# Four-layer attention chain on one core: feature maps, reciprocals, first keys and three residuals computed in another way, with new instruction orders

## The chip, the core and the metric

One Trainium2 chip, one of its cores. A core has five engines with a queue of instructions each: PE (TensorE, matrix products into PSUM), ACT (ScalarE), DVE (VectorE), POOL (GpSimd) and SP (SyncE, which here only issues transfers). They run side by side and wait for each other by semaphores; each takes its own instructions strictly in order. The metric is the time of one launch on the device, in microseconds (us), as the median of several runs.

## The reference

Four residual layers, A, B, A, B, over a sequence of 2048 rows of 512 numbers (bf16), 32 heads of 16. Both layers of a kind use the same weights.

```python
def A(x, wqkv, wo):                     # linear attention
    q, k, v = split(x @ wqkv)           # heads of 16
    phi = lambda t: where(t > 0, t + 1, exp(t)) + 1e-6
    pq, pk = phi(q), phi(k)
    kv = einsum("bhsd,bhse->bhde", pk, v)
    z = einsum("bhsd->bhd", pk)
    num = einsum("bhqd,bhde->bhqe", pq, kv)
    den = einsum("bhqd,bhd->bhq", pq, z)[..., None] + 1e-6
    return (num / den) @ wo

def B(x, wqkv, wo):                     # causal attention, window of 256
    q, k, v = split(x @ wqkv)
    p = softmax(where(mask, q @ k.T * 0.25, -1e9))
    return (p @ v) @ wo

x = x + A(layernorm(x)); x = x + B(layernorm(x))
x = x + A(layernorm(x)); x = x + B(layernorm(x))
```

## The kernel before

The 2048 rows lie in SBUF as 16 tiles of 128 rows (xres, bf16). The work falls into five stretches that overlap at their edges:

1. the first layer's keys: each tile is normalised (`norm`: statistics, mean and variance on DVE, `eps` and `pow` on POOL, the scaled tile `xn` on DVE), transposed by PE for tiles 0 to 4 and by a transfer for the others, multiplied by the weights of keys and queries (`a_k`, `a_q`), and sent through the feature map `phi`;
2. the first middle stretch: for each tile the end of layer A (`a_out`, residual `resid`), the layer norm, layer B's queries, keys and values (`b_qkv`, `b_v`), scores (`b_scores`, `b_first`, `b_far`), exponentials on ACT, masks, the product with the values (`b_values`), the output product (`b_out`), the residual, the next layer norm, and the second layer A's keys and values;
3. the change-over (`barrier`): the sums over all tiles (`a_kv`), the remaining queries, the matrix M, and for each group G of four tiles the denominators `den`, their reciprocals `rec`, and `spread`, a product that repeats each reciprocal over the 16 columns of its head;
4. the second middle stretch, the same as the first with the last layer B; it writes the finished tiles out;
5. the tail: the last two tiles' values, output products, residuals and stores (`b_last` for tile 15).

Nothing in the program looks for parallelism while it runs. A planner was run beforehand, and its result is the packed `TABLE`: one order of all instructions, the engine of each instruction that could run on two (a copy out of PSUM may be on ACT or DVE, a far mask on DVE or POOL, a store on POOL or SP), and the PSUM bank of each product. `place` unpacks it, and `synchronise` derives the semaphore waits. The keys and parameters in the text (`PAR`) have no further effect on the order. The eight PSUM banks are reused all the time: a product waits until the readers of the bank's last content are done.

The parts that the change touches:

- `phi` has two forms. The plain one: `E` (exponential, ACT, PSUM to tE), `E1` (minimum with 1, plus 1e-6, DVE), `phi` (plus 1 and maximum, DVE, which reads the product from PSUM and tE). The form with `near`: ACT makes two passes over the product, `E` and `R` (plus 1, into XQ), and DVE takes the maximum `mx` of two SBUF tiles. `BY_ACT` lists the query tiles with the second form: 0 to 6 for the first layer A, 4 to 8 for the second.
- the product of a query tile with its spread reciprocals: `pqd` on DVE straight from PSUM, or, for the groups in `COPIED`, a copy `sc` into tE (ACT or DVE) and a product `pm` of two SBUF tiles on DVE. `COPIED` holds group 0 of the first and groups 0 and 1 of the second layer A.
- the keys of layer B are stored twice, once with the odd and once with the even rows zero. For most tiles `bke` copies them out of PSUM and two transfers `kd` place them; for the tiles in `NEAR` (tile 0 of both layers B) two passes `kz` over PSUM write them directly, each scaled by a column of zeros and ones.
- `tok` is the product of a tile of rows with a matrix of 512 columns, four matmuls of 512 columns in two halves; `resid` adds it to xres on DVE. `WHOLE`, which would put the residual into the product, is empty.
- `LAST` says how many of the last tiles of a layer B have their attention output transposed by PE rather than by a transfer: 1 in the first layer B, 2 in the second.

Of the kernel before, what the change touches and what calls it, by code (L numbers as in the profile page):

```python
# [9 lines left out]
ALU = mybir.AluOpType  # L10

P = 128
# [223 lines left out]
class Plan:  # L236
# [173 lines left out]
    def tok(self, name, t, lhs, rhs, rd, key, whole=False):  # L410
# [3 lines left out]
        if whole:  # L414
            self.pe("id", lambda e: e.matmul(K.ps(ps), K.ident[:], K.xres[:, t, :], start=True, stop=False), key - 0.01, 1, 512, rd=[("xres", t), ("ident",)], ps=[ps])
        for h in range(2):
            def put(e, h=h):
                m = None
                for c in (2 * h, 2 * h + 1):
                    m = e.matmul(K.ps(ps), lhs(c), rhs(c), start=c == 0 and not whole, stop=c == 3)  # L420
                return m
            self.pe(name, put, key - 0.001 * h, 2, 512, rd=rd, ps=[ps])
# [417 lines left out]
    def b_out(self, j, key, by_pe, whole=False):  # L840
# [4 lines left out]
        if whole:  # L845
            return po
        self.resid(j, po, key + 0.05)

    def b_last(self, j, key):
# [4 lines left out]
        for h in range(2):  # L854
# [10 lines left out]
            for n in range(2) if h else [None]:  # L865
                cs = slice(0, D) if n is None else slice(256 * n, 256 * n + 256)

                def put(e, h=h, cs=cs):
                    m = None
                    for f in (h, h + 2):  # L870
                        m = e.matmul(K.ps(po)[:, cs], K.oT[:, s, f, :], K.wBo[:, f, cs], start=f == 0, stop=f == 3, skip_group_check=True)
                    return m

                self.pe("bout", put, key + 0.1 * h + 0.01 * (n or 0), 2, cs.stop - cs.start, rd=[("oT", s, h), ("wBo",)], ps=[po])
        for n in range(2):
            cs = slice(256 * n, 256 * n + 256)
            self.on("DVE", "res", lambda e, cs=cs: e.tensor_tensor(K.xres[:, j, cs], K.ps(po)[:, cs], K.xres[:, j, cs], ALU.add), key + 0.2 + 0.1 * n, dve(256), rd=[("xres", j)], wr=[("xres", j, n)], ps=[po])
# [291 lines left out]
```

## Time and profile before

| | |
|---|---|
| median of 3 runs | 412.12 us (411.43 to 413.2) |
| the profiled execution | 412.6 us, span 410.8 us |
| instructions in the span | 17540 |
| busy: PE / DVE / ACT / POOL | 386.9 / 344.5 / 352.8 / 122.4 us |
| granted PE clock | full in every slice |
| exponentials and copies of scores, ACT (line 686) | 216 instructions, 198.9 us |
| chain that ended last, by engine | PE 51%, ACT 34%, DVE 9%, DMA 3% |

The span is what the hardware profiler saw; the execution's own time is 1.8 us longer. Busy times of ACT, DVE and POOL are the union of their instructions' times. Matmuls are pipelined, so one matmul's listed time is longer than the step from one to the next, and PE's busy time alone does not say how full PE is. The chain is followed backwards from the last instruction, at each step to what released it or to the instruction ahead of it on its engine.

### The profile page before, as it was taken

The numbers are of one execution on the slowest core, as the hardware profiler recorded it, in microseconds if no ns is written. First come the engines' busy times: TensorE is split into PE (matmuls) and PEld (weight loads), VectorE is DVE, ScalarE is ACT, GpSimd is POOL, SyncE is SP. The second block draws the span as 40 slices with busy tenths as digits, with TensorE's granted clock in tenths as the row PEclk, the third lists the DMA queues.
The fourth block names the chain that finished last, engine by engine and source line by source line (L and its number), as shares of the span: only waits on it lengthen the run. The fifth ranks groups of instructions, "written<-read, shape, count | busy, mean of one in ns | idle before, by whom it ended". The sixth has DMA issues, their size and how long they took to land.

```text
span 410.8 us, 17540 instructions
## 1 busy us (share of the span) xinstructions
PE 386.9 (94%) x7668; PEld 260.3 (63%) x7742; DVE 344.5 (84%) x807; ACT 352.8 (86%) x448; POOL 122.4 (30%) x216
## 2 busy tenths in 40 slices
PE   7999999999999999999999999999999988999896
PEld 3654676766575576566567777586757755566674
DVE  6997799989998899888887789997899688857585
ACT  4654659998999999999998357999999999999993
POOL 4576653111252331320503203303113304303020
PEclk9999999999999999999999999999999999999999
DMA  7495114443243435353222100344314821561751
GB/s 249 101 217 144 49 34 115 120 70 90 56 106 74 119 77 107 81 119 82 68 41 57 27 2 2 105 109 81 102 44 122 122 66 41 120 127 56 168 107 42
DMA packets 66596, 37.19 MB, mean 91 GB/s; under 512 B 47640, under 2 KB 61848, under 8 KB 66520
## 3 DMA queue, kind: packets, MB, share of 16 engines
q1 hardware_dynamic: 66032, 34.75, 37.0%
q8 instruction: 61, 1.00, 1.1%
q0 software_dynamic: 480, 1.31, 1.0%
q14 instruction: 15, 0.12, 0.1%
q10 hardware_dynamic: 8, 0.00, 0.0%
HBM read 6.29 MB, written 2.10 MB: 20 GB/s over the span
## 4 chain that ended last, share of the span: by engine, by line
PE 51%; ACT 34%; DVE 9%; DMA 3%; issue 2%; SPq 1%; POOL 1%
ACT pb L686 20%; PE ps L420 18%; PE ps L434 10%; PE ps L822 10%; PE ps L676 5%; ACT pb L801 5%; ACT vp L686 4%; PE ps L501 3%; ACT tE L444 2%; DMA wA<-in_A_wqkv_dram 2%; DMA xT<-xn 1%; DVE xres L604 1%; DVE stats L374 1%; ACT pb L721 1%; PE ps L477 1%
## 5 line engine op out<-in xcount | busy, mean ns | idle before, releaser
L686 ACT ACTIVATE pb<-ps 128x1024 bf16<-128x1024 f32 (+2 forms) x216 | 198.9, 1020 | 5.2 <-PE ps L676 3.9
L822 PEld LDWEIGHTS ps<-vB,pb 128*128 128x128 bf16 x2560 | 77.7, 96 | 12.3 <-DVE pb L694 3.6
L822 PE MATMUL ps<-vB,pb 128*128 128x34 bf16 x2560 | 83.5, 177 | 0.6 <-POOL pb L772 0.3
L434 PE MATMUL ps<-xT,wBp 128*128 128x128 bf16 x1024 | 69.0, 219 | 1.7 <-ACT tE L444 0.6
L434 PEld LDWEIGHTS ps<-xT,wBp 128*128 128x128 bf16 x1024 | 58.5, 98 | 13.7 <-issue 4.4
L379 POOL TENSOR_SCALAR ve<-mv 128x1 f32<-128x1 f32 x63 | 16.7, 265 | 154.7 <-DVE mv L375 152.7
L444 ACT ACTIVATE tE<-ps 128x512 bf16<-128x512 f32 x64 | 38.6, 612 | 27.1 <-PE ps L420 11.2
L772 POOL TENSOR_SCALAR_AFFINE_SELECT pb<-pb 128x1024 bf16<-128x1024 bf16 x30 | 34.4, 1146 | 71.4 <-DVE pb L694 23.8
L676 PE MATMUL ps<-XQ,kB 32*128 32x256 bf16 (+3 forms) x992 | 48.0, 267 | 3.3 <-ACT pb L754 0.7
L604 DVE TENSOR_TENSOR xres<-ps,xres 128x512 bf16<-128x512 f32 x63 | 43.0, 684 | 6.7 <-PE ps L420 6.3
L420 PE MATMUL ps<-wA,XQ 128*128 128x512 bf16 x174 | 45.6, 379 | 2.2 <-issue 0.6
L374 DVE BATCH_NORM_STATS2 stats<-xres 128x6 f32<-128x512 bf16 x64 | 43.5, 685 | 2.8 <-DMA xres<-in_A_x_dram 2.2
L694 DVE TENSOR_TENSOR pb<-pb,tri 128x512 bf16<-128x512 bf16 (+1 forms) x108 | 41.5, 396 | 3.3 <-ACT pb L686 3.1
L801 ACT ACTIVATE pb<-ps 128x1024 bf16<-128x1024 f32 x42 | 41.4, 1059 | 1.1 <-PE ps L792 0.9
L380 POOL TENSOR_TENSOR rs<-ve,negh 128x1 f32<-128x1 f32 x64 | 37.8, 591 | 8.3 <-DVE ve L377 3.0
L434 PE MATMUL ps<-XQ,wA 128*128 128x128 bf16 x512 | 35.4, 219 | 0.3 <-DMA wA<-in_A_wqkv_dram 0.3
L434 PEld LDWEIGHTS ps<-XQ,wA 128*128 128x128 bf16 x512 | 30.7, 98 | 7.3 <-DMA wA<-in_A_wqkv_dram 0.8
L420 PE MATMUL ps<-wBv,xT 128*128 128x512 bf16 x110 | 31.4, 380 | 2.6 <-issue 1.0
L676 PEld LDWEIGHTS ps<-XQ,kB 32*128 32x128 bf16 x992 | 15.0, 92 | 29.5 <-ACT pb L686 7.5
L420 PE MATMUL ps<-M,XQ 128*128 128x512 bf16 x113 | 30.7, 380 | 2.3 <-ACT vp L686 0.4
L420 PE MATMUL ps<-wBo,oT 128*128 128x512 bf16 x105 | 28.8, 380 | 2.8 <-issue 1.0
L686 ACT ACTIVATE vp<-ps 128x1024 bf16<-128x1024 f32 (+2 forms) x32 | 26.7, 928 | 1.5 <-PE ps L676 1.5
(126 smaller groups left out, 551.6 us busy)
## 6 DMA issues: line engine op xcount, KB each, us to landing
vB<-vS SPq DMA_DIRECT2D x64, 136.0 KB, 2.7
kB<-vp SPq DMA_DIRECT2D x60, 128.0 KB, 2.3
wA<-in_A_wqkv_dram SPq DMA_DIRECT2D x3, 512.0 KB, 5.5
out_dram<-xres POOLq DMA_DIRECT2D x10, 128.0 KB, 2.8
xres<-in_A_x_dram SPq DMA_DIRECT2D x2, 512.0 KB, 5.1
pb<-in_B_wqkv_dram SPq DMA_DIRECT2D x1, 1024.0 KB, 5.8
xres<-in_A_x_dram SPq DMA_DIRECT2D x3, 256.0 KB, 5.5
out_dram<-xres SPq DMA_DIRECT2D x5, 128.0 KB, 2.7
```

What stands on the lines that cost most here:

```text
L374: self.on("DVE", "stats", lambda e: e.bn_stats(K.stats[:, t, :], x()), key, dve(512), rd=rd, wr=[("stats", t)], **held)
L380: self.pow = self.on("POOL", "pow", lambda e: e.tensor_tensor(K.rs[:, t, :], K.ve[:, t, :], K.negh[:], ALU.pow), key + 0.03, (640, 690), r ...
L420: m = e.matmul(K.ps(ps), lhs(c), rhs(c), start=c == 0 and not whole, stop=c == 3)
L434: m = e.matmul(K.ps(ps)[:, f * P:(f + 1) * P], w(c, f), xT(c), start=c == 0, stop=c == 3)
L444: self.on("ACT", "E", lambda e: e.activation(K.tE[:, s, :], K.ps(ps), ACT.Exp, bias=0.0), key, act(512), wr=[("tE", s)], ps=[ps])
L604: self.on("DVE", "res", lambda e: e.tensor_tensor(K.xres[:, t, :], K.ps(po), K.xres[:, t, :], ALU.add), key, dve(512), rd=[("xres", t)], w ...
L676: m = e.matmul(K.ps(ps[gq])[:, ns * i:ns * i + ns], K.kB[rows, j % 4, 2 * f + b, :, :], K.XQ[rows, f, q:q + ns], start=True, stop=True, ti ...
L686: return e.activation(out(2 * h, 2, ns), i, ACT.Exp, bias=0.0, scale=0.25)
L694: return e.tensor_tensor(x, x, K.tri[:, 0, sh:64].unsqueeze(1).unsqueeze(1).to_broadcast([P, 4, n, 64 - sh]), ALU.mult)
L772: return e.affine_select(out=x, in_=x, compare_op=ALU.is_ge, fill=0.0, base=-2, pattern=[[0, 16], [-2, 64]], channel_multiplier=1)
L801: return e.activation(far(h), i, ACT.Exp, bias=0.0, scale=0.25)
L822: m = e.matmul(K.ps(ps)[:, 34 * u:34 * u + 34], K.P((b // 2) % rp)[:, gq, f, o:o + P], K.vB[:, (b // 2) % 4, b % 2, r, :], start=i == 0, s ...
```

## The change

Five edits in the text:

- `BY_ACT` becomes empty: all 64 feature maps take the plain form.
- `COPIED` becomes empty: every spread reciprocal is read from PSUM by `pqd`.
- `NEAR` becomes empty: tile 0's keys go the way of the others, `bke` and two transfers, in both layers B.
- the residual of tiles 13, 14 (by `WHOLE`) and of half of tile 15 in the last layer is added inside the product, by a matmul of the identity with xres that accumulates into the same bank, and a plain copy `rs` writes the sum back. For tile 15 the other half stays an addition on DVE, the copy is ordered behind it, and one store of 128 KB takes the place of two of 64 KB.
- `LAST` of the second layer B falls from 2 to 1: tile 14's attention output is transposed by a transfer.

`TABLE` is replaced: the order, the engine of each free instruction and all banks are new. Counted over the program, ACT loses 19 of 447 instructions and DVE 13 of 806; five far masks move from DVE to POOL, and PE has three matmuls more for the residuals and four transposing ones fewer.

```diff
--- before.py
+++ after.py
@@ -215,13 +215,13 @@
 LATE = 5
 KEEP = 0
 MASKS = 0
-WHOLE = {2: (), 3: ()}
+WHOLE = {2: (), 3: (13, 14)}
 FIRST = {2: 0, 3: 0}
-BY_ACT = {2: (0, 1, 2, 3, 4, 5, 6), 3: (4, 5, 6, 7, 8)}
-COPIED = {2: (0,), 3: (0, 1)}
-LAST = {2: 1, 3: 2}
+BY_ACT = {2: (), 3: ()}
+COPIED = {2: (), 3: ()}
+LAST = {2: 1, 3: 1}
 PART = (2, 3)
-NEAR = (0,)
+NEAR = ()
 PACK = {3: (9, 10, 11, 12, 13, )}
 QUAD = ()
 SUMMED = ()
@@ -411,15 +411,18 @@
 
         K = self
         ps = Tile(1, K.cls)
-        if whole:
-            self.pe("id", lambda e: e.matmul(K.ps(ps), K.ident[:], K.xres[:, t, :], start=True, stop=False), key - 0.01, 1, 512, rd=[("xres", t), ("ident",)], ps=[ps])
         for h in range(2):
             def put(e, h=h):
                 m = None
                 for c in (2 * h, 2 * h + 1):
-                    m = e.matmul(K.ps(ps), lhs(c), rhs(c), start=c == 0 and not whole, stop=c == 3)
+                    m = e.matmul(K.ps(ps), lhs(c), rhs(c), start=c == 0, stop=c == 3 and not whole)
+                if whole and h:
+                    m = e.matmul(K.ps(ps), K.ident[:], K.xres[:, t, :], start=False, stop=True)
                 return m
-            self.pe(name, put, key - 0.001 * h, 2, 512, rd=rd, ps=[ps])
+            if whole and h:
+                self.pe(name + "i", put, key - 0.001 * h, 3, 512, rd=rd + [("xres", t), ("ident",)], ps=[ps])
+            else:
+                self.pe(name, put, key - 0.001 * h, 2, 512, rd=rd, ps=[ps])
         return ps
 
     def feat(self, name, t, w, xT, rd, key):
@@ -591,16 +594,17 @@
                 self.on("DVE", "pqd", lambda e, x=x, b=bc[tg]: e.tensor_tensor(x(), K.ps(b).rearrange("p (f n) -> p f n", f=4), x(), ALU.mult), k + 0.3 + 0.01 * tg, dve(512), rd=[("XQ", t)], wr=[("XQ", t)], ps=[bc[tg]])
 
 
-    def a_out(self, t, key, whole):
+    def a_out(self, t, key):
         K = self
         x = lambda f: K.XQ[:, f, t * P:(t + 1) * P]
-        po = self.tok("aout", t, x, lambda f: K.M[:, f, :], [("XQ", t)] + [("M", f) for f in range(4)], key + 0.1, whole)
+        po = self.tok("aout", t, x, lambda f: K.M[:, f, :], [("XQ", t)] + [("M", f) for f in range(4)], key + 0.1)
+        self.resid(t, po, key + 0.15)
+
+    def resid(self, t, po, key, whole=False):
+        K = self
         if whole:
-            return po
-        self.resid(t, po, key + 0.15)
-
-    def resid(self, t, po, key):
-        K = self
+            self.copy("rs", po, lambda: K.xres[:, t, :], lambda: K.ps(po), key, 512, wr=[("xres", t)])
+            return
         self.on("DVE", "res", lambda e: e.tensor_tensor(K.xres[:, t, :], K.ps(po), K.xres[:, t, :], ALU.add), key, dve(512), rd=[("xres", t)], wr=[("xres", t)], ps=[po])
 
     def b_qkv(self, t, s, key, key2):
@@ -842,9 +846,7 @@
         s = j % 2
         self.transpose("oT", lambda: K.o[:, s, :], lambda: K.oT[:, s, :, :], [("o", s, 0), ("o", s, 1)], [("oT", s)], key - 0.15, by_pe)
         po = self.tok("bout", j, lambda f: K.oT[:, s, f, :], lambda f: K.wBo[:, f, :], [("oT", s), ("wBo",)], key, whole)
-        if whole:
-            return po
-        self.resid(j, po, key + 0.05)
+        self.resid(j, po, key + 0.05, whole)
 
     def b_last(self, j, key):
 
@@ -869,13 +871,17 @@
                     m = None
                     for f in (h, h + 2):
                         m = e.matmul(K.ps(po)[:, cs], K.oT[:, s, f, :], K.wBo[:, f, cs], start=f == 0, stop=f == 3, skip_group_check=True)
+                    if not h:
+                        m = e.matmul(K.ps(po)[:, 256:512], K.ident[:], K.xres[:, j, 256:512], start=False, stop=False, skip_group_check=True)
                     return m
 
-                self.pe("bout", put, key + 0.1 * h + 0.01 * (n or 0), 2, cs.stop - cs.start, rd=[("oT", s, h), ("wBo",)], ps=[po])
-        for n in range(2):
-            cs = slice(256 * n, 256 * n + 256)
-            self.on("DVE", "res", lambda e, cs=cs: e.tensor_tensor(K.xres[:, j, cs], K.ps(po)[:, cs], K.xres[:, j, cs], ALU.add), key + 0.2 + 0.1 * n, dve(256), rd=[("xres", j)], wr=[("xres", j, n)], ps=[po])
-            self.on("SP", "out", lambda e, cs=cs: e.dma_start(K.out[0, j * P:(j + 1) * P, cs], K.xres[:, j, cs]), key + 0.3 + 0.1 * n, (520, 2400), rd=[("xres", j, n)])
+                if h:
+                    self.pe("bout", put, key + 0.1 * h + 0.01 * (n or 0), 2, cs.stop - cs.start, rd=[("oT", s, h), ("wBo",)], ps=[po])
+                else:
+                    self.pe("boutj", put, key, 3, 512, rd=[("oT", s, h), ("wBo",), ("xres", j), ("ident",)], ps=[po])
+        self.on("DVE", "res", lambda e: e.tensor_tensor(K.xres[:, j, 0:256], K.ps(po)[:, 0:256], K.xres[:, j, 0:256], ALU.add), key + 0.2, dve(256), rd=[("xres", j)], wr=[("xres", j, 0)], ps=[po])
+        self.copy("rs", po, lambda: K.xres[:, j, 256:512], lambda: K.ps(po)[:, 256:512], key + 0.3, 256, rd=[("xres", j)], wr=[("xres", j, 1)])
+        self.on("SP", "out", lambda e: e.dma_start(K.out[0, j * P:(j + 1) * P, :], K.xres[:, j, :]), key + 0.4, (520, 2400), rd=[("xres", j, 0), ("xres", j, 1)])
 
     def phase(self, ph):
 
@@ -898,7 +904,7 @@
 
         def front(t):
             k = base + t
-            po = self.a_out(t, k - par["k_ao"], t in WHOLE[ph])
+            po = self.a_out(t, k - par["k_ao"])
             self.norm(t, k - par["k_ao"] + 0.3, t % ring, lambda: K.xT[:, t % ring, :, :], [("xT", t % ring)], t < max(par["pe_first"], FIRST[ph]), po)
             self.b_qkv(t, t % ring, k - par["k_q"], k - par["k_kv"])
 
@@ -952,60 +958,59 @@
 TABLE = (
...
 )
```

More of the change, by code (lines that the diff above doesn't have):

```diff
@@ L1007 @@
[L1007 to L1008 removed]
+    r"c-qxh1GFv4lFd*?=Cf_vwr$(CZQHhO+qP|W_e0y9bI$Fa_5b|tp7;Crnzg3xJ*TRoB6jT95t-{$Bx6hzgGLM+FwqT}7$&AkWvq#1Qk%#owi#m5nCJeLA8OK?",
+    r"I3}+dW}f-D=81pm^O+ZZxJhU7n-M0x>1ba13?`l_V2YYfCcY_XI-BVxqse5t7&S9YSCiDtG?|SvyUj?`%_K0hOb)ZsbT`RN7L(JgGJ8yNGux~-g-lj6$Mi6T",
+    r"O;3~1tT8FfDAV7pHHl0vv(7X%)l4sQ)-*E%Om5TM>^0%dIn&!DF?mdBlijp1qfH-k-i$FV%>|R#WHT4dShLUEH?2%%Gtl%k(ae5R%#1U0%>gsWj5n=K4b#sI",
@@ L1009 @@
+    r"SWl2k&>qk(tnknP1^gr!iX14+hR6om64u$^8VJp0U>W?@6bw-aL~>BfKs%MglnjnX;30*&761ih4XwanIib-HoB3b?fu)3@RzX++p~eI+DX{Q@tql_@Wc^J{",
+    r"pwPkyrVf36i-iCK37e;2w?kto7`FOC(-F2TzywyT3AB;%zW@>cD^U",
 )
```

102 lines of the change are left out of this document (48 added, 54 removed).

## The prediction

> **What bounds the kernel now.** I read four views in this order: busy time of each engine, busy time by stretch (columns: engine busy times with instruction counts, granted clock, DMA share, GB/s), the groups of PE within one stretch, and what ACT waited for.
>
> ```profile
> PE 386.9 (94%) x7668; PEld 260.3 (63%) x7742; DVE 344.5 (84%) x807; ACT 352.8 (86%) x448; POOL 122.4 (30%) x216
> ```
> ```profile
> 0.00:62.90 62.90, 59.65 (x600) 35.48 (x610) 53.64 (x135) 33.80 (x58) 37.16 (x80) 1.00 0.50 133
> 62.90:218.80 155.90, 148.92 (x3087) 98.93 (x3117) 138.13 (x320) 151.17 (x176) 40.88 (x69) 1.00 0.39 87
> 218.80:259.00 40.20, 39.32 (x674) 29.75 (x681) 34.22 (x81) 25.29 (x47) 10.94 (x19) 1.00 0.12 29
> 259.00:403.00 144.00, 134.91 (x3231) 93.38 (x3253) 114.70 (x267) 141.18 (x167) 32.93 (x49) 1.00 0.44 95
> 403.00:410.80 7.80, 4.05 (x89) 2.75 (x86) 3.83 (x9) 1.36 (x3) 0.54 (x1) 0.99 0.17 53
> ```
>
> The cuts are at the first exponential of each layer B, the last but a few of the first, and the last of the second. In the middle stretches ACT works 151.17 of 155.90 us and 141.18 of 144.00; in the opening and the change-over only 33.80 of 62.90 and 25.29 of 40.20. There PE shows 95% and 98%, which pipelining makes doubtful, so I count its work, first by the step between matmuls (chain of waits: start, us, what), then by the matmuls of 20 to 30 us:
>
> ```profile
> 28.98 0.86 PE ps L501 x4
> 48.03 0.89 PE ps L434 x16
> ```
> ```profile
> L420 PE MATMUL ps<-wA,XQ 128*128 128x512 bf16 x20 | 5.5, 379 | 0.0
> L501 PE MATMUL ps<-vp 128*128 128x512 bf16 x17 | 4.6, 379 | 0.1
> L434 PE MATMUL ps<-XQ,wA 128*128 128x128 bf16 x32 | 2.4, 219 | 0.0
> ```
>
> A 512-column matmul steps by 0.86/4 = 0.215 us, a 128-column one by 0.89/16 = 0.056. So 37 x 0.215 + 32 x 0.056 = 9.7 of these 10 us are products: the opening is bound by PE. The Trainium skill ("TensorE: Matmul & The Clock Gate", Back-to-back issue gap) gives about 131 ns per 512-column matmul in a sustained stream and calls 216 ns the isolated gap. By 131 the same 10 us would hold 6.6 us of products, PE would not bind, and an ACT cut there would count (rival A); the row says 215 ns within a stream, so I keep PE as the bound.
>
> In the middle stretches ACT's idle time is mostly waits for scores:
>
> ```profile
> ACT pb L686 <- PE ps L676: 2.6, 6, 0.6
> ```
> ```profile
> ACT vp L686 <- PE ps L676: 1.5, 3, 0.7
> ```
>
> The first row is of 62.9 to 218.8 us, the second of 259 to 403. So the kernel is bound by PE, ACT, PE, ACT, and a short tail.
>
> **The change part by part.** The pieces that go or come have these groups (mean ns of one behind the comma):
>
> ```profile
> L446 ACT ACTIVATE XQ<-ps,one 128x512 bf16<-128x512 f32 x12 | 8.3, 688 | 0.2
> L449 DVE TENSOR_TENSOR XQ<-XQ,tE 128x512 bf16<-128x512 bf16 x12 | 4.9, 416 | 0.1
> L451 DVE SCALAR_TENSOR_TENSOR XQ<-ps,tE 128x512 bf16<-128x512 f32 x20 | 13.6, 682 | 0.2
> L407 ACT ACTIVATE tE<-ps 128x512 bf16<-128x512 f32 x8 | 4.7, 604 | 1.6 <-PE ps L579 1.6
> L589 DVE TENSOR_TENSOR XQ<-tE,XQ 128x512 bf16<-128x512 bf16 x12 | 4.7, 416 | 0.3 <-ACT tE L407 0.2
> L407 DVE CAST tE<-ps 128x512 bf16<-128x512 f32 x4 | 2.7, 677 | 0.0
> L591 DVE TENSOR_TENSOR XQ<-ps,XQ 128x512 bf16<-128x512 f32 x20 | 12.7, 683 | 2.2 <-PE ps L579 2.2
> L624 ACT ACTIVATE kB<-ps,par 128x512 bf16<-128x512 f32 x4 | 3.4, 838 | 0.0
> L627 ACT ACTIVATE vp<-ps 128x512 bf16<-128x512 f32 x7 | 5.4, 777 | 0.7 <-PE ps L434 0.6
> L407 ACT ACTIVATE vS<-ps 128x512 bf16<-128x512 f32 x6 | 4.3, 712 | 0.0
> L407 ACT ACTIVATE XQ<-ps 128x512 bf16<-128x512 f32 x9 | 5.4, 605 | 0.6 <-PE ps L434 0.6
> L407 ACT ACTIVATE vp<-ps 128x512 bf16<-128x512 f32 x4 | 2.5, 616 | 0.5 <-PE ps L420 0.5
> L773 DVE TENSOR_TENSOR pb<-pb,tri 128x1024 bf16<-128x1024 bf16 x20 | 15.2, 766 | 0.1
> L772 POOL TENSOR_SCALAR_AFFINE_SELECT pb<-pb 128x1024 bf16<-128x1024 bf16 x30 | 34.4, 1146 | 71.4 <-DVE pb L694 23.8
> ```
>
> *Feature maps.* 12 `R` go from ACT (8.3 us), 12 maxima of 416 ns become 12 `phi` of 682: DVE +3.2 us. Seven are in the opening, five in the change-over, where PE is the bound: ACT's 8.3 us there are worth nothing by themselves. The cover of DVE's +1.9 us (7 x 0.266) is thin: DVE is the other full engine from 10 to 30 us.
>
> ```profile
> 10.00:20.00 10.00, 9.78 (x98) 6.57 (x98) 9.84 (x29) 6.05 (x12) 5.56 (x16) 1.00 0.43 106
> 20.00:30.00 10.00, 9.95 (x85) 5.55 (x84) 9.75 (x31) 5.75 (x10) 7.21 (x17) 1.00 0.91 218
> ```
>
> DVE has room outside these 20 us (53.64 - 9.84 - 9.75 = 34.1 us of work in 42.9), and PE still has later queries to do meanwhile, so I take 0, with ends 0 and +1.9.
>
> *Spread reciprocals.* 8 copies go from ACT (4.7 us) and 4 from DVE (2.7); 12 products of 416 ns become 683: DVE +3.2 - 2.7 = +0.5. All lie where PE is the bound: 0. In the change-over the new list puts fewer DVE instructions ahead of tile 1's `xn` but more ahead of tile 2's; these cancel.
>
> *Tile 0's keys.* Four `kz` of 838 ns become two `bke` of 777 on ACT, whose bank comes free 0.9 us earlier. Who waited for the `kz`:
>
> ```profile
>   PEld ps L579: 0.6, 1
> ```
>
> That is the spread's weight load, once, for 0.6 us; PE had other products behind it, so I take half as gain (ends 0 and -0.6). In exchange `kd` transfers must land before the first score. SP issues them behind tile 1's transpose (first layer B) and straight away (second); the list keeps 10 x 0.215 + 32 x 0.056 = 3.9 us of PE work between the second `kd` and the first score in the first layer B, and 2 x 0.215 + 32 x 0.056, with a transpose and a spread 2.7 us, in the second. A `kd` lands in 2.3 us (below), so both are covered, the second narrowly (+0.6 at the most).
>
> *Engine choices.* In the first middle stretch ACT gets one `bke` and one copy of values more and one `bve` less: 0.777 + 0.616 - 0.712 = 0.7 us, less the overlap of neighbours some +0.5, and ACT is the bound: +0.5. In the second, two `bke` and one `bqe` go and one `bve` comes: 2 x 0.777 + 0.605 - 0.712 = 1.4, with overlap -1.2. Five far masks move from DVE (766 ns) to POOL (1146 ns), all in the second middle stretch, where POOL works 32.93 of 144.00 us: hidden, the `eps` and `pow` queued behind a mask included, ends 0 and 5 x 0.4 = +1.9.
>
> *The loads at the start.* The new list issues tiles 4-5 ahead of tiles 2-3 and both ahead of the key weights, which move from fourth to fifth on SP.
>
> ```profile
> 5.42 0.69 DVE L374 BATCH_NORM_STATS2 stats<-xres 128x6 f32<-128x512 bf16 x1 [0.23 <-DMA xres<-in_A_x_dram]
> 7.15 1.03 PE L420 MATMUL ps<-wA,XQ 128*128 128x512 bf16 x4
> 8.29 1.29 DVE L374 BATCH_NORM_STATS2 stats<-xres 128x6 f32<-128x512 bf16 x2 [0.26 <-DMA xres<-in_A_x_dram]
> 9.79 0.62 PE L434 MATMUL ps<-XQ,wA 128*128 128x128 bf16 x8 [0.32 <-DMA wA<-in_A_wqkv_dram]
> ```
>
> Tile 2 landed at 5.42 and, behind the key weights, tile 4 at 8.29; changed about, the key weights end near 8.3, and DVE does tile 4's statistics (0.69) ahead of tile 1's `xn`. The first product moves from 7.15 to about 8.4. Most of that falls into PE's wait for the query weights at 9.79, which are behind the same bytes as before; two key products (1.72) then end at about 10.2, and the identity fill and a transpose remain. PE is full afterwards, so it stays: +0.4, ends 0 and +1.3.
>
> *The tail.* Two of the three residual copies are on DVE, as dear as the addition (a 512-column DVE read of PSUM is 677 to 683 ns in every row above); the third, on ACT, is ordered behind DVE's half. PE: +0.215 (tile 14) + 0.11 (tile 15) - 0.22 (four transposing matmuls) = +0.1. Transfers of 390 to 411 us, and `kd`:
>
> ```profile
> kB<-vp SPq DMA_DIRECT2D x60, 128.0 KB, 2.3
> out_dram<-xres SPq DMA_DIRECT2D x2, 128.0 KB, 2.8
> out_dram<-xres SPq DMA_DIRECT2D x2, 64.0 KB, 1.6
> oT<-o SPq DMA_TRANSPOSE x2, 3.4
> 401.53 0.42 DVE L835 TENSOR_TENSOR o<-ps,rc 128x256 bf16<-128x256 f32 x1
> 405.14 0.81 PE L420 MATMUL ps<-wBo,oT 128*128 128x512 bf16 x3
> ```
>
> Tile 14's output is complete at 401.95. Its transpose by transfer lands at 405.4 if it takes 3.4 us and before 405 if it is quicker, and its product, with tile 15's second transpose and product queued behind on PE, begins at 405.1 today: +0.3, ends 0 and +0.6. The last store leaves with the second half, as before, but has 128 KB: between 0 and 2.8 - 1.6 = +1.2, I take +0.6. Tail: +1.0.
>
> Sum: +0.4 (start) - 0.3 (bank) + 0.5 - 1.2 (ACT in the middle) + 1.0 (tail) = +0.4 on the profiled 412.6 us. The median is 0.5 below that execution, so 412.12 + 0.4 = 412.5 us.
>
> What I can't price is the order itself. Put side by side, PE's lists have almost the same matmuls ahead of each exponential, while DVE's is shuffled throughout.
>
> **Rivals.** *A, faster:* shorter ACT lists at the change-overs, and banks read sooner, bring scores in time. For it: ACT is idle for 155.90 + 144.00 - 151.17 - 141.18 = 7.6 us in the middle, 4.1 of it in the two rows of waits; between tile 0's transposed copy and the first exponential of the second layer B, ACT's list falls from 13 instructions to 10. Against it: PE's count, and that DVE's work hardly falls. With two fifths of the 7.6 gone: 412.5 - 3.0 = 409.5. By the 131 ns of the Trainium skill's page named above, this would be the likelier course.
>
> *B, slower:* DVE's new order makes scores late. PE waits in order for DVE's copies and masks, and each late score leaves ACT idle: nine waits of 4.1 us now, 0.46 each. For it: DVE works 138.13 of 155.90 us in the first middle stretch, so it has little room to catch up. Against it: PE's unchanged list, and DVE at 80% in the second. It decides from five more waits (2.1 us); a doubling gives 412.5 + 4.1 = 416.6.
>
> *C, no use of the identity product:* the residuals gain nothing and the tail alone is longer. It is within my forecast.
>
> **How the numbers follow.** 0.5% is 2.06 us, about what a measurement of this kernel can tell from no change. My forecast, within it: 0.43, own range 410.4 to 414.2 (the ends of the start, the masks and the tail partly add up, and partly cancel against ACT). A: 0.29, 406.5 to 410.0. B: 0.28, 414.2 to 420. The range that leaves out 0.1 at either side is 407.5 to 417.5.
>
> **What would show it.** In the profile after: no `R`, `sc` or `kz`; ACT at about 28 us of the opening and 21 of the change-over, with both stretches no shorter; the first key product near 8.4 us; ACT's work 140 us from the second first exponential on; the last store's landing nearer 2.8 than 1.6 us. I am wrong by A if the first exponentials come at 61 and 255 us or earlier, and by B if ACT's waits for scores exceed 7 us.

## The result and the profile after

The changed kernel takes 415.94 us (median of 4 runs, 415.5 to 416.43), the kernel before in the same session 411.85 us (4 runs, 411.43 to 413.2): a ratio of 1.0081, with a 95% interval of 1.0059 to 1.0104. The forecast was 412.5 us and "no change"; the change costs 0.8%. That is inside the whole range (407.5 to 417.5), outside the forecast's own range (410.4 to 414.2), and in the range that was given to rival B. The profiled execution took 415.88 us with a span of 414.2 us, 3.4 us more than the span of before.

The first view of the changed kernel is its busy time by engine, the second its busy time by stretch, cut at the same events as before (columns as in the prediction):

```profile
PE 396.6 (96%) x7741; PEld 260.9 (63%) x7741; DVE 345.8 (83%) x794; ACT 341.9 (83%) x429; POOL 127.9 (31%) x221
```
```profile
0.00:63.31 63.31, 60.35 (x609) 35.68 (x610) 54.80 (x133) 27.29 (x48) 36.92 (x79) 1.00 0.54 133
63.31:219.00 155.69, 152.78 (x3080) 98.90 (x3078) 138.66 (x317) 151.10 (x176) 40.15 (x69) 1.00 0.40 89
219.00:260.02 41.02, 40.85 (x717) 30.03 (x716) 35.06 (x77) 21.60 (x39) 10.82 (x19) 1.00 0.12 29
260.02:405.13 145.11, 138.19 (x3258) 93.35 (x3257) 114.30 (x262) 140.77 (x165) 38.97 (x54) 1.00 0.42 95
405.13:414.20 9.07, 4.46 (x88) 2.92 (x84) 2.94 (x8) 1.15 (x3) 1.08 (x2) 1.00 0.21 60
```

ACT has 10.9 us less to do (352.8 to 341.9), and the kernel is slower. ACT fell from 33.8 to 27.3 us in the opening and from 25.3 to 21.6 in the change-over, as forecast, and neither became shorter.

To see where the 3.4 us arise I number the 312 exponentials of the two layers B in order of time and take, from the traces, when the k-th starts. The table gives the kernel before in us, and for the changed kernel and the kernels of the experiments (below) how much later each comes. Number 0 ends the opening, 156 the change-over, and 311 is the last.

| | 0 | 156 | 240 | 276 | 292 | 298 | 311 | span |
|---|---|---|---|---|---|---|---|---|
| before, us | 62.89 | 258.98 | 343.63 | 374.96 | 388.23 | 393.50 | 402.58 | 410.8 |
| after | +0.42 | +1.04 | +0.03 | +0.81 | +0.81 | +1.94 | +2.18 | +3.4 |
| tile 14 by PE | +0.55 | +0.80 | -0.17 | +0.61 | +0.63 | +1.75 | +2.06 | +2.3 |
| old end order | +0.44 | +1.04 | +0.08 | +1.12 | +1.14 | +2.15 | +2.54 | +4.0 |
| key weights third | +0.87 | +1.26 | +0.28 | +1.15 | +1.17 | +1.30 | +2.04 | +3.2 |
| old order from 156 | +0.80 | +1.17 | +0.70 | +0.81 | +0.81 | +1.20 | +1.24 | +1.5 |
| old order from 240 | +0.02 | +1.22 | +0.25 | +1.83 | +1.85 | +1.86 | +2.02 | +2.3 |
| the same, old tail | +0.07 | +0.20 | -0.76 | +0.66 | +0.68 | +0.98 | +1.20 | +1.1 |
| before, new order 156 to 240 | -0.31 | +0.75 | +0.14 | +1.83 | +1.85 | +1.85 | +1.75 | +1.7 |
| features undone | +1.39 | +2.11 | +1.09 | +1.92 | +1.92 | +3.48 | +3.76 | +4.8 |
| keys undone | +1.11 | +2.21 | +1.19 | +2.01 | +2.02 | +3.65 | +4.01 | +5.1 |
| reciprocals undone | +1.74 | +4.81 | +4.02 | +4.64 | +4.65 | +4.78 | +6.20 | +7.4 |
| all three undone | +4.48 | +11.34 | +11.01 | +11.80 | +11.82 | +12.94 | +12.96 | +14.5 |
| two edits in old order | +3.51 | +3.60 | +6.85 | +6.96 | +6.96 | +7.30 | +7.14 | +7.1 |

Single profiles scatter: six kernels with the same instructions up to exponential 0 reach it between 62.91 and 63.69 us, two with the old ones at 62.89 and 62.58; the means, 63.27 and 62.74, differ by 0.5. At exponential 156 the same six rows lie between +0.20 and +1.22, with a mean of 0.91. So a difference of less than about 1 us between two rows says nothing in these columns. What a row gains or loses within a later stretch is steadier: from 156 to 240 eight rows that have the new order there gain 0.96 to 1.02 us each.

In this one profile (second row) the changed kernel is 0.4 us late after the opening and 1.0 at the start of the second layer B, makes that up by exponential 240, loses 0.8 again by 276, 1.1 between 292 and 298, and 1.2 behind the last exponential.

The start, and the waits of ACT for scores in the two middle stretches (first row of the waits 62.9 to 219 us, the others 259 to 405; engine, what, releaser: us, times, longest):

```profile
8.77 1.90 PE L418 MATMUL ps<-wA,XQ 128*128 128x512 bf16 x8 [1.03 <-DMA wA<-in_A_wqkv_dram]
```
```profile
ACT pb L690 <- PE ps L680: 2.6, 7, 0.6
```
```profile
ACT vp L690 <- PE ps L680: 2.1, 5, 0.6
ACT pb L690 <- PE ps L680: 1.3, 3, 0.7
```

These rows have 15 waits of 6.0 us; before there were nine of 4.1. The timeline of the changed kernel shows where the new ones are (start, busy us, instructions run together, idle time before them), and the third fence what PE did ahead of the longest:

```profile
359.99 1.08 ACT L758 ACTIVATE pb<-ps 128x512 bf16<-128x512 f32 x2 [0.24 <-PE ps L749]
367.20 2.86 ACT L690 ACTIVATE vp<-ps 128x1024 bf16<-128x1024 f32 x3 [0.50 <-PE ps L680]
370.28 1.09 ACT L758 ACTIVATE vp<-ps 128x512 bf16<-128x512 f32 x2 [0.22 <-PE ps L749]
391.35 3.35 ACT L690 ACTIVATE pb<-ps 128x1024 bf16<-128x1024 f32 x4 [0.37 <-PE ps L680]
395.43 5.18 ACT L690 ACTIVATE pb<-ps 128x1024 bf16<-128x1024 f32 x6 [0.74 <-PE ps L680]
```
```profile
393.87 0.20 PE L826 MATMUL ps<-vB,pb 128*128 128x34 bf16 x2
394.80 0.20 PE L826 MATMUL ps<-vB,pb 128*128 128x34 bf16 x2 [0.72 <-issue]
394.85 0.20 PE L826 MATMUL ps<-vB,vp 128*128 128x34 bf16 x2
394.98 0.40 PE L680 MATMUL ps<-XQ,kB 32*128 32x256 bf16 x8
```

The first three idle times, together 0.96 us, cover the 0.78 us lost between 240 and 276. The last, 0.74, stands behind a gap of 0.72 us inside a group of value products that has no wait in it: "issue" means that the profile shows nothing that PE waited for.

The tail. The first fence is from the timeline of the kernel before, the second from the chain of the changed kernel that ended last, the third from its timeline:

```profile
402.30 0.66 ACT L686 ACTIVATE vp<-ps 128x256 bf16<-128x256 f32 x2 [0.66 <-PE ps L676]
404.81 0.27 PE L860 MATMUL ps<-ident,o 128*128 128x128 bf16 x2
407.64 0.83 SPq L878 DMA_DIRECT2D out_dram<-xres  x2
```
```profile
403.93 4.03 DMA oT<-o
```
```profile
403.49 0.41 DVE L839 TENSOR_TENSOR o<-ps,rc 128x256 bf16<-128x256 f32 x1
404.47 0.66 ACT L690 ACTIVATE vp<-ps 128x256 bf16<-128x256 f32 x2 [0.27 <-PE ps L680]
408.01 1.04 PE L418 MATMUL ps<-wBo,oT 128*128 128x512 bf16 x4 [0.87 <-DMA oT<-o]
409.10 0.27 PE L862 MATMUL ps<-ident,o 128*128 128x128 bf16 x2
411.36 0.34 SPq L884 DMA_DIRECT2D out_dram<-xres  x1
```

Tile 14's transposition by transfer takes 4.03 us from issue to landing. PE waits 0.87 us for it at 408.01 with tile 15's second transpose (409.10) behind. The last store (128 KB) is issued at 411.36 and lands 1.7 us later, at 413.07; before, the second of two stores of 64 KB was issued at 408.10 and landed 1.6 us later, at 409.68. In both traces 1.1 us of semaphore instructions follow until the span ends. The row is from the transfers of the changed kernel from 404 us on:

```profile
out_dram<-xres SPq DMA_DIRECT2D x1, 128.0 KB, 1.7
```

### The profile page after: what moved, and what is told of

It reads as the page before. It is cut to its first block, busy times and chain, and to the rows that moved or that the text cites. A ratio compares the mean times of both kernels' runs of the same rounds, so it can differ in the third digit from the quotient of the medians.

```text
span 414.2 us, 17594 instructions
## 1 busy us (share of the span) xinstructions
PE 396.6 (96%) x7741; PEld 260.9 (63%) x7741; DVE 345.8 (83%) x794; ACT 341.9 (83%) x429; POOL 127.9 (31%) x221
## 4 chain that ended last, share of the span: by engine, by line
PE 60%; ACT 25%; DVE 6%; DMA 5%; SPq 1%; issue 1%; POOL 1%; POOLq 0%
PE ps L418 22%; ACT pb L690 14%; PE ps L437 13%; PE ps L826 12%; PE ps L680 6%; ACT vp L690 4%; PE ps L504 3%; ACT pb L805 3%; DVE XQ L594 2%; DMA wA<-in_A_wqkv_dram 1%; DMA xT<-xn 1%; DMA vB<-vS 1%; PE ps L796 1%; DMA oT<-o 1%; PE ps L480 1%
## 5 line engine op out<-in xcount | busy, mean ns | idle before, releaser
L776 POOL TENSOR_SCALAR_AFFINE_SELECT pb<-pb 128x1024 bf16<-128x1024 bf16 x33 | 38.2, 1156 | 56.5 <-DVE pb L698 23.9
L418 PE MATMUL ps<-wA,XQ 128*128 128x512 bf16 x192 | 49.8, 380 | 1.7 <-DMA wA<-in_A_wqkv_dram 1.0
L608 DVE TENSOR_TENSOR xres<-ps,xres 128x512 bf16<-128x512 f32 x61 | 41.5, 684 | 5.6 <-PE ps L418 5.2
L418 PE MATMUL ps<-wBv,xT 128*128 128x512 bf16 x128 | 34.8, 380 | 0.1
L418 PE MATMUL ps<-M,XQ 128*128 128x512 bf16 x128 | 34.0, 381 | 0.6 <-ACT vp L690 0.4
L418 PE MATMUL ps<-wBo,oT 128*128 128x512 bf16 x124 | 33.3, 380 | 1.2 <-DMA oT<-o 0.9
L418 PEld LDWEIGHTS ps<-wA,XQ 128*128 128x128 bf16 x192 | 16.5, 97 | 20.0 <-DMA wA<-in_A_wqkv_dram 1.4
```

What stands on the lines that cost most here:

```text
L418: m = e.matmul(K.ps(ps), lhs(c), rhs(c), start=c == 0, stop=c == 3 and not whole)
L776: return e.affine_select(out=x, in_=x, compare_op=ALU.is_ge, fill=0.0, base=-2, pattern=[[0, 16], [-2, 64]], channel_multiplier=1)
```

## The experiments

My theory behind the forecast was that the named edits cost or gain nothing where PE is the bound, and that the order decides the rest. The rivals were that the edits themselves cost time, that DVE's order makes scores late (rival B), and, once the trace was seen, that PE's gap comes from its instruction stream.

All experiments keep the code and rewrite the packed table of order, engines and banks. Where a diff shows a list, it is a part of one engine's order.

**One. The three ACT edits undone in the new order.**

```diff
-BY_ACT = {2: (), 3: ()}
-COPIED = {2: (), 3: ()}
-NEAR = ()
+BY_ACT = {2: (0, 1, 2, 3, 4, 5, 6), 3: (4, 5, 6, 7, 8)}
+COPIED = {2: (0,), 3: (0, 1)}
+NEAR = (0,)
```

> The changed kernel with three of its named edits undone inside its own order: the 12 linear feature copies (688 ns each) are back on ACT with their maxima on DVE, the 12 copies of the spread reciprocals (8 on ACT by the changed kernel's neighbours, 4 on DVE) are back, and tile 0's keys are again made by two scaled copies of 838 ns in place of a copy and two transfers. Every other instruction keeps its place. Theory 'order': these edits lie where PE is the bound and carry nothing, so the time is that of the changed kernel, 415.9 within 0.8 us, although ACT is busy some 11 us longer (about 353 instead of 342). Theory 'edits': the one-pass feature map, the direct products or the key transfers hold banks longer or come late, so undoing them gives back at least 1.5 us (414.4 or less). Theory 'the cuts help': without them it is slower, 417.5 or more.

Measured: 427.28 us against 412.79, ratio 1.0353 (1.0333 to 1.0372), 2.7% above the changed kernel's 1.0081. Only the third expected case is left, and it gave no more than a lower bound of 1.6 us: putting the work back costs 11 us, 4.1 of it in the opening and 6.2 more by exponential 156, both stretches where PE was counted as the bound. So "ACT's work there is worth nothing" cannot be right for these instructions in these places. Experiments nine to eleven take the three apart.

**Two. The old order at the end.**

```diff
 PE, from tile 14's last value product on:
-values 14 (heads of f = 3), scores 15 (f = 2, 3; banks 3 4 6 7), bout 13, scores 15 (odd rows)
+scores 15 (f = 2, 3; banks 1 2 6 7), values 14 (f = 3), bout 13, scores 15 (odd rows)
```

> The changed kernel with the old order from the second scores of tile 15 in the last layer on: the scores of heads 2 and 3, half 0, of tile 15 stand ahead of the second half of tile 14's last value product again and write banks that earlier exponentials left, instead of standing behind it and in the banks of the exponential just before. Theory 'late scores at the end': the exponentials of tile 15 lose 0.9 us there in the changed kernel (lag to the kernel before grows from 0.64 to 1.52 us); the repair takes 0.7 to 1.2 us off, to about 414.9. Theory 'instruction stall': the 0.72 us for which PE waited for nothing in that value product comes from elsewhere and stays, and the time falls by less than 0.3 us.

Measured: 416.07 us against 412.79, ratio 1.0070 (1.0042 to 1.0099): no change to speak of. The row "old end order" keeps the whole loss between 292 and 298, and the gap is still there:

```profile
395.02 0.20 PE L826 MATMUL ps<-vB,pb 128*128 128x34 bf16 x2 [0.73 <-issue]
```

So the place of tile 15's scores does not cause it. The first expected case fell; that the gap stays, the second, came true.

**Three. Tile 14's transposition by PE again.**

```diff
-LAST = {2: 1, 3: 1}
+LAST = {2: 1, 3: 2}
```

> The changed kernel with tile 14's transposition on PE, as before the change, in place of a transfer; all else is kept. Theory 'tail transfer': the transfer takes 4.03 us and PE waits 0.87 us for it with tile 15's transpose behind, so 0.6 to 1.0 us go, to about 415.1, and the stretch behind the last exponential falls from 9.07 to some 8.2 us. Theory 'store': the tail is longer because of the single last store of 128 KB, and less than 0.3 us goes.

Measured: 415.12 us against 412.79, ratio 1.0061 (1.0044 to 1.0077); the span falls by 1.1 us and the stretch behind the last exponential from 9.07 to 8.08. The two medians alone could not show a difference of 0.8 us, since their intervals overlap. The tail itself does, because it is steady from trace to trace: from the start of the last exponential to the end of the span it takes 9.3 to 9.8 us in the seven profiles with the transfer, 8.5 in the three that have the transposition on PE and else the new tail, and 8.1 to 8.2 in the four with the old tail. So the tail transfer costs 0.9 to 1.0 us of the 1.23.

```profile
405.02:413.10 8.08, 4.35 (x91) 3.07 (x89) 2.94 (x8) 1.75 (x4) 1.08 (x2) 0.93 0.15 51
```

What is left, 8.08 against 7.84, is the identity products and the single store.

**Four. The key weights loaded third.**

```diff
 SP:
-x0, x1, x4, x2, wAk, wAq
+x0, x1, wAk, x4, x2, wAq
```

> The changed kernel with the key weights issued third, ahead of both loads of later rows, in place of fifth. Theory 'start': the first key product comes about 1.5 us earlier than at 8.77 and the first exponential of layer B 0.4 us earlier than at 63.31, and that stays to the end: 415.5. Theory 'covered': PE then waits longer for the query weights or for the rows that now land later, and the first exponential stays within 0.15 us or comes later.

Measured: 415.55 us against 412.79, ratio 1.0077 (1.0054 to 1.0100). The first key product comes at 9.13 us, later than 8.77. DVE's list has tile 4's statistics ahead of tile 1's scaled copy; tile 4 now lands 1.5 us later, and PE, whose list has tile 1's transpose ahead of the key product, waits for that copy:

```profile
6.62 0.69 DVE L374 BATCH_NORM_STATS2 stats<-xres 128x6 f32<-128x512 bf16 x1 [1.42 <-DMA xres<-in_A_x_dram]
8.68 0.40 PE L395 MATMUL ps<-ident,vp 128*128 128x128 bf16 x4 [1.48 <-DVE vp L381]
9.13 1.24 PE L418 MATMUL ps<-wA,XQ 128*128 128x512 bf16 x5
```

One load moved alone gains nothing, because the lists behind it were made for the other arrival. One thing I did not expect: in this run the gap in PE's value products is absent, and with it the loss between 292 and 298 (+1.17 to +1.30), although PE's program is the same. The saving does not last: from 298 to 311 this run loses 0.74 us where the changed kernel loses 0.24.

**Five and six. The old order for the second middle stretch, from its start and from exponential 240 on.**

```diff
-LAST = {2: 1, 3: 1}
+LAST = {2: 1, 3: 2}
 all engines:
-the new order to the end
+the new order up to the cut, then the remaining instructions in the old order
```

> The changed kernel's order up to the first scores of the second layer B, and from there the old order, with the change's edits kept but for tile 14's transposition, which is on PE again. Theory 'second stretch's order': the changed kernel enters this stretch 1.0 us late (first exponential at 260.02 against 258.98), loses 1.1 us more in it by its own order and 1.2 in the tail; with the old order there only the entry and the identity products of the tail (0.2) remain, so 1.2 us over the kernel before. Theory 'edits and entry': the late scores come from what the stretch is handed, and the time stays 2.0 us or more over the kernel before, as with the transposition alone mended (415.12 against 412.79).

> As the run that takes the old order from the second layer B's first scores, but the cut is later: the changed kernel's order up to the 240th exponential (of 312), where it has made up its lag (+0.03 us), and the old order from there. Theory 'last third': the new order is good up to here and loses 1.7 us only behind it (late scores at 360 to 370 and at 391 to 404 us), so the time is 0.3 us over the kernel before. Theory 'borrowed time': the new order is ahead at this place only because it has left DVE or PE work for later; then the old order meets that work and the gain of 1.0 us is lost again, giving 1.0 us or more over the kernel before.

Measured: 414.01 us against 412.6, ratio 1.0041 (1.0026 to 1.0057), with the cut at the start; 414.83, ratio 1.0060 (1.0042 to 1.0078), with the cut at 240. The first agrees with "second stretch's order" (1.4 us over the kernel before where 1.2 was expected). It is 0.8 us under the transposition mended alone, which the overlapping intervals do not tell from nothing; in the table that lies between 292 and 311, where this row loses 0.43 us and the other 1.43. With the old order the lag goes from 1.17 to 0.70 by 240 and stays there up to 292; only 0.4 is lost between 292 and 298. The second agrees with "borrowed time": the new order is ahead at 240 and the old order behind it pays at once, in one wait:

```profile
347.31 7.45 ACT L690 ACTIVATE pb<-ps 128x1024 bf16<-128x1024 f32 x8 [1.40 <-PE ps L680]
```

The changed kernel pays for the same lead in the three waits at 360 to 370 us. A seam between two lists may cost something by itself, and no run separates that from the work put off; the changed kernel has no seam, and there 0.78 of the 1.02 us are lost again by 276.

**Seven. As six, with the old tail.**

```diff
-WHOLE = {2: (), 3: (13, 14)}
+WHOLE = {2: (), 3: ()}
 b_last: two residual additions and two stores of 64 KB, no boutj
```

> As the run with the cut at the 240th exponential, with the tail as before the change: the residuals of tiles 13, 14 and 15 are additions on DVE again, without identity products, and the last store is two stores of 64 KB. Theory 'identity product costs 0.2': 0.1 to 0.3 us less than the run with these edits kept. Theory 'store': two smaller stores land earlier and 0.5 us or more is gained.

Measured: 414.02 us against 412.6, ratio 1.0042 (1.0026 to 1.0058), 0.8 us under run six. Most of that is not the tail: its stretch from the last exponential on is 0.4 us shorter (411.9 - 404.15 = 7.75 against 413.1 - 404.98 = 8.12), the rest lies before it, within the scatter. So identity products and one large store cost 0.2 to 0.4 us together, 0.1 of it the store's later landing (1.7 us against 1.6); a gain of the identity product is not seen anywhere.

**Eight. The kernel before with the new order between 156 and 240.**

```diff
 all engines, from the second layer B's first scores to exponential 240:
-the old order
+the new order, with its banks and choice of engines
```

> The kernel before, with none of the named edits; only between the first scores of the second layer B and the 240th exponential does it follow the changed kernel's order, banks and choice of engines (four far masks more on POOL and one fewer, two key copies from ACT to DVE, one value copy from DVE to ACT). Theory 'the new order is better there': 0.7 to 1.0 us under the kernel before. Theory 'borrowed time' or 'only a lag made up': the same as the kernel before within 0.3 us.

Measured: 414.38 us against 412.6, ratio 1.0046 (1.0030 to 1.0062): slower, worse than either expectation. It has the same wait of 1.40 us at its cut (at 347.20), and 1.14 us at the entry. What looked like a gain of 1.0 us up to 240 is work put off, as far as these two seams show, and it is no piece that can be taken over as it stands.

**Nine to eleven. Each ACT edit undone by itself in the new order.**

```diff
-BY_ACT = {2: (), 3: ()}
+BY_ACT = {2: (0, 1, 2, 3, 4, 5, 6), 3: (4, 5, 6, 7, 8)}
```

> The changed kernel with the 12 linear feature copies back on ACT, each right behind its exponential, and the 12 maxima in place of the combined DVE step; nothing else moves but one constant of GpSimd, set early. ACT gets 8.3 us of work, DVE loses 3.2, all of it where PE was counted as the bound. Theory 'covered': the time is that of the changed kernel within 0.8 us. Theory 'in the way': from the run with three edits undone, whose exponentials of the feature maps fell back by 0.7 us in the opening and 1.2 us in the change-over before the copies and keys came, the time rises by 1.5 to 2.5 us. Theory 'one-pass form holds banks': it falls by 1 us or more.

```diff
-NEAR = ()
+NEAR = (0,)
```

> The changed kernel with tile 0's keys made by two scaled copies of 838 ns on ACT again, in place of a copy of 777 ns and two transfers, in both layers B. Theory 'bank' (the prediction's -0.3 us for the edit): 0 to 0.8 us slower than the changed kernel, by 0.9 us for which the second spread or other work waits for the bank. Theory 'serial section': in the run with three edits undone PE waited 0.9 us for these copies in the opening; undone alone they cost 1.5 us or more over both layers. Theory 'transfers late': the transfers were on the path, and it is 0.5 us or more faster.

```diff
-COPIED = {2: (), 3: ()}
+COPIED = {2: (0,), 3: (0, 1)}
```

> The changed kernel with the 12 spread reciprocals copied out of PSUM again (on the engines of the kernel before), each copy standing right behind its spread or behind the product that frees its buffer; the products of a group of four follow the old order among themselves. Theory 'covered': within 0.8 us of the changed kernel. Theory 'serial section': denominators, reciprocals, spread, copy, product, first scores follow one another with little beside them, so each copy that PE or DVE waits for adds 0.6 us, 2 us or more in all; of the 11.4 us of the run with three edits undone most would be here.

Measured against 411.9: features 417.48 (ratio 1.0130, 1.0101 to 1.0158), keys 417.62 (1.0140, 1.0110 to 1.0170), reciprocals 419.70 (1.0188, 1.0161 to 1.0215). Over the changed kernel's 1.0081 these are about 2.0, 2.4 and 4.4 us, each by some 1.5 us uncertain when the two intervals are put together; the sum is 8.8 of the 11.2 that undoing all costs. By exponential 156, where the undone edit is the only difference, the three are 1.2, 1.3 and 3.9 us behind the mean of the six rows above. What PE waited for says why (waits of PE: the first fence the changed kernel's opening; then the opening with features undone, the opening with keys undone, the opening and the change-over with reciprocals undone):

```profile
PE ps L1087 <- DVE kB L1079: 1.2, 1, 1.2
PE ps L418 <- DMA wA<-in_A_wqkv_dram: 1.0, 1, 1.0
PE ps L395 <- DVE vp L381: 0.4, 1, 0.4
PE ps L418 <- DVE mv L375: 0.2, 1, 0.2
```
```profile
PE ps L504 <- DVE vp L454: 0.7, 2, 0.4
PE ps L437 <- ACT M L407: 0.3, 1, 0.3
```
```profile
PE ps L582 <- ACT kB L628: 0.9, 1, 0.9
```
```profile
PE ps L437 <- ACT M L407: 0.6, 1, 0.6
PE ps L550 <- ACT M L407: 0.5, 1, 0.5
```
```profile
PE ps L418 <- ACT M L407: 1.3, 1, 1.3
PE ps L437 <- DVE tE L407: 0.9, 1, 0.9
PE ps L716 <- ACT XQ L407: 0.4, 1, 0.4
```

With the feature copies back, PE waits 0.7 us in the sums (L504) for feature maps of keys on DVE, and 0.3 us for a copy of M that stands behind them on ACT. With the two scaled key copies back, the spread (L582) waits 0.9 us for their bank. With the copies of the reciprocals back, the copies of M and of the first queries, which stand behind them on ACT, are late, and so is a reciprocal's copy on DVE; PE stands still for them for 3.7 us in all. PE is the busiest engine in these stretches, and yet single copies on ACT hold it up: its list stands still at the product that waits for one. For features and keys a part of the 2.0 and 2.4 us is not the edit: 0.3 us is a longer gap in the value products (1.0 against 0.72 us), and some of the later start is scatter.

**Twelve. Two of the edits made in the old order.**

```diff
-COPIED = {2: (0,), 3: (0, 1)}
-NEAR = (0,)
+COPIED = {2: (), 3: ()}
+NEAR = ()
 DVE: E1 and phi of query tile 8 and the product of tile 7 some ten places earlier
```

> The kernel before, its order kept on PE, ACT, GpSimd and SP, with two of the named edits made: spread reciprocals straight from PSUM and tile 0's keys by transfers. On DVE three instructions stand some ten places earlier (the feature map of query tile 8 and the product of tile 7), because a bank is now freed by the product. Theory 'covered': the time of the kernel before within 0.5 us. Theory 'serial section': the copies and scaled keys were on the path, so it is 1 us or more faster than the kernel before. Theory 'holds banks': direct products free their banks later than copies, and it is slower by 1 us or more.

Measured: 419.06 us against 411.9, ratio 1.0169 (1.0144 to 1.0194). Taking ACT's copies away costs 7 us here; the two edits were not tried one by one in this order. PE waits for the direct products on DVE (L591), twice in the opening and once early in the second layer B:

```profile
49.10 0.39 PE L547 MATMUL ps<-wAo,pqd 128*128 128x512 bf16 x1 [1.17 <-DVE XQ L591]
54.58 1.04 PE L420 MATMUL ps<-M,XQ 128*128 128x512 bf16 x4 [1.56 <-DVE XQ L591]
```
```profile
PE ps L420 <- DVE XQ L591: 2.4, 1, 2.4
```

"Holds banks" is borne out: in the old order DVE has other work ahead of the product, and a copy on ACT freed the bank meanwhile. The first wait in the trace is M's product, which does not read the reciprocals' product and so can wait only for its bank. The three waits are 5.1 of the 7.2 us; where the rest arises was not followed. Together with runs one and nine to eleven this is the main finding: undone in the order made for them the edits cost some 1 to 4 us each, two of them made in the other order cost 7 us, and edits and order changed together cost 0.8%, or 3.4 us. In these runs the pieces were put into a finished list by hand. No run plans a new order around a single edit, so what an edit is worth in an order made for it stays open.

No kernel of this study is faster than the kernel before.

## Why the prediction was right or wrong

**The bound.** Right in what it forecast: no `R`, `sc` or `kz`, ACT at 27.3 and 21.6 us (28 and 21 forecast), both stretches no shorter. Wrong as a reason. The prediction costed each of these edits at nothing because PE is the bound and ACT has room; the runs show some 1 to 4 us for each when it is put back alone. Room on an engine covers a step only where its place in the list is not one that PE waits for. That the changed kernel is only 0.9 us late after both stretches (the mean of six rows at exponential 156), and not several, is most likely because its order had been made together with the edits; this is argued from run twelve, not shown.

The chain of the changed kernel still shows four 512-column products in 0.86 us:

```profile
365.85 0.86 PE ps L418 x4
```

That is 0.215 us each, and in all 14 traces no two such products in a row start closer together than that. The 131 ns that the Trainium skill ("TensorE: Matmul & The Clock Gate", Back-to-back issue gap) gives for a sustained stream is seen in no run here. Rival A, which that figure would have made likelier, did not come.

**The start, +0.4.** Right: the first key product came at 8.77 us (8.4 forecast), the first exponential 0.42 later, 0.5 on average over profiles. The reason given, the later key weights, is only half of it: with them loaded earlier the product waits for tile 1's copy instead.

**Tile 0's keys, -0.3.** Not seen in the sum. That the spread waits for the bank of the scaled copies was right in its place, and is 0.9 us when the copies are put back in the new order; their whole effect there is 1.3 us by exponential 156 and about 2.4 us in the time.

**Choice of engines, +0.5 and -1.2.** This is the first term that failed. ACT's work fell only from 141.20 to 140.77 us in the second middle stretch and from 151.18 to 151.10 in the first. In the second stretch the durations of the single instructions add up to 1.8 us less, and the overlap of neighbours takes 1.3 of it, where the prediction took off 0.2. The lead that the changed kernel has at exponential 240 looks like the -1.2, but runs six and eight show it as work put off, and 0.96 us of waits at 360 to 370 give most of it back.

**Far masks, 0.** POOL's work in that stretch rose from 32.95 to 38.97 us. No row ties a wait to it; it was not tried by itself.

**The tail, +1.0.** Near in sum (+1.23) and wrong in its parts. The transposition by transfer was given +0.3 and costs 1.0: it took 4.03 us where 3.4 was taken from the median of two others, and the 0.6 us between them is what was missing. Its later issue, at 403.93 in place of about 402, is no part of that, since tile 14's output is late by as much as the last exponential. The store was given +0.6 and costs 0.1: the 1.6 us for 64 KB was right, but the 2.8 us for 128 KB were the median of two others, and the last one landed in 1.7. So that sign, a landing nearer 2.8 than 1.6 us, failed. The identity products, +0.1, fit what remains.

**The order, not priced.** This is the second and larger failure: between exponentials 292 and 311 the changed kernel loses 1.4 us (0.81 to 2.18), for which the sum had nothing. The eight rows that have the new order there lose 0.9 to 2.0 us, the five other rows with the old order -0.1 to 0.5. What in the new order causes it is found only in part: a gap in PE's value products, of which more below, and later scores where that gap is missing. By terms, the sum of the forecast was +0.4; the trace has +0.4 at the start, +0.6 by 156, -0.2 by 292, +1.4 by 311 and +1.2 in the tail.

**The rivals.** B forecast 416.6 us and the kernel takes 415.94, but its mechanism carries only a part. Its mark was more than 7 us of waits for scores; the same rows have 6.0. Of the 1.9 us that were added, 0.74 follow PE's gap, which DVE has no share in, and the tail's 1.2 is not in B at all. C, no use of the identity product, agrees with the 0.2 to 0.4 us of runs three and seven.

## What to carry to other kernels

Where every engine has a fixed list, an edit has no price of its own: copies that the one order holds without visible waits cost some 1 to 4 us when they were put into the other, so a step is to be costed by who stands behind it in the lists of PE and of the engine that runs it, not by how busy that engine is. A lead in the middle of a stretch is to be compared at its end, since it may be work put off. In a tail, the issue-to-landing time of the very transfer that is last counts, not the median of its kind: here the medians said 3.4 and 2.8 us, and the two transfers took 4.03 and 1.7.

## What the hardware showed

PE may be standing still for its own instructions; what follows is a correlation in traces, and no run set out to test it. The gap in the value products appears in six of the eight profiles that follow the new order to the last tiles, always within half a microsecond of the same place, and in none of the six that take the old order there (none over 0.13 us without a releaser). The instruction queue of the page moves 61 blocks:

```profile
q8 instruction: 61, 1.00, 1.1%
```

That is 16 KB each; 256 instructions a block, as the Trainium skill ("Runtime: NRT & Kernel Launch", Instruction fetch mechanics) has it, would make 15,600, and PE has 7741 products and as many weight loads. The start of the blocks' transfers, from the packet records of the traces, in us from exponential 292, beside the gap:

| | blocks start at | PE resumes at | gap |
|---|---|---|---|
| after | -7.4, -1.3, +3.1 | +5.75 | 0.72 |
| old end order | -7.4, -1.4, +3.1 | +5.65 | 0.73 |
| tile 14 by PE | -7.4, -1.4, +3.1 | +5.75 | 0.72 |
| all three undone | -7.5, -1.2, +3.6 | +5.81 | 0.50 |
| features undone | -7.3, -1.4, +3.6 | +5.96 | 1.01 |
| keys undone | -7.4, -1.3, +3.7 | +6.07 | 1.04 |
| key weights third | -8.4, -4.4, +1.7 | | none |
| reciprocals undone | -8.4, -4.4, +1.7 | | none |

Where the block starts at +1.7 there is no gap; where it starts at +3.1 or later PE resumes 2.2 to 2.7 us behind its start. So the gap goes with a late block, in eight profiles of eight. In the six kernels with the old order the block starts at +1.6 to +2.9, and PE does not stop there without a releaser. Smaller gaps of that kind fit too: 0.31 us with all three undone (PE resumes at +1.59) and 0.13 us in runs seven and twelve (+1.44 and +1.46) stand 2.3 to 2.8 us behind the start of the block before (-1.2, -0.9 and -0.8), though run five with a block at -1.2 has none. The same section of the Trainium skill calls the cost of a block boundary mostly hidden; if the gaps are that cost, it was 0.5 to 1.0 us here, with ACT idle behind it. Why the block before started at -1.3 in one group and at -4.4 in the other stays open: it was not tried, and the traces show only that both occur with the same PE program. The two runs without it lose 0.1 us between 292 and 298, the changed kernel 1.1. But up to 311 they lose a further 0.7 and 1.4 us, the changed kernel 0.2: over the whole end it is 0.9 and 1.6 us without the gap against 1.4 with it. So what the time would gain without the gap stays open.
